# A linear-attention block followed by a multiplicative feed-forward block: PSUM banks split four and four, kv in quarters of the array, the second factor's pieces and the last block rearranged

## The chip, the cores and the metric

The kernel runs on one core of a Trainium2 chip. The time is device microseconds of one execution. Three runs of the kernel before gave 779.88, 779.91 and 781.03 us; the median is 779.91 us. The profile is of one further execution, whose instructions span 776.9 us (778.64 us as that run was timed). All sums here are made against that span.

## What is computed

For each of 8 batches and 8 heads, with 576 tokens and a head dimension of 64:

```
kv  = k^T v                      # 64 x 64 per head, summed over 576 tokens
o   = q kv                       # 576 x 64
x   = o / sqrt(mean(o*o) + 1e-6) * g_norm
```

The heads are put side by side, so that `x` is 4608 tokens by 512. Then, with w1 and w2 of 512 x 1024, w3 of 1024 x 1024 and w_out of 1024 x 512:

```
a = x w1;  b = x w2;  h = (a*b) w3;  out = h w_out
```

All inputs and the result are float32 in value; the weights come in a wider format and are converted on the chip.

## The kernel before, in words

**Weights first.** `w3 w_out` doesn't depend on x, so the kernel multiplies it once (`turn_w3`, L579, and `fold_chunk`, L592; about 16 to 85 us of the span) and keeps the 1024 x 512 product in `w3o_sb`. While that runs, batch 0 of attention runs between the chunks.

**Groups of tokens.** 512 of each batch's 576 tokens form a group of their own; the 64 left over of all eight batches form a ninth group. The groups run in the order 0 to 6, 8, 7 (L1085). For each group T the gate products `x w1` and `x w2` are made in four passes (`gates`, L742), and then the projection by `w3o_sb`. Group 0 projects with one level of Winograd's scheme for 2 x 2 blocks (`project`, L766); every later group with two levels (`project_twice`, L854), which needs the second factor's blocks in seven pieces, with their own sums.

**The second factor's pieces.** `prepare_b` (L795) makes these seven pieces once, during the gates of group 1, four VectorE subtractions for each, staged in one of the two output tiles `o_sbs`, and stores each by two DMAs into a scratch tensor in DRAM (`w3o_l2`). Piece 6 is stored once more by itself, unsummed, for use at the very end (L799). `load_b` (L823) fetches pieces again, for every group, into one of three stream buffers. `between` (L1089) is called twice in each gate pass and makes two pieces each time.

**One pass of gates** is `winograd` (L610): seven products of 4 float32 matmuls each, in PSUM banks r1, r2 and r3. ScalarE copies banks out (`keep`, L628) as `p1`, `p5`, `u2`, `u3`; VectorE adds banks to those and multiplies the two halves (`multiply`, L747). Their order is: r1 for p1, r2 for p5, r1 again for u2; `between`; r2 again for block c12; r1 again for u3; r3 for c11; `between`; r1 a fourth time for c21. So r1 is given back only when c21 has been read. For c21, ScalarE copies half of the bank (L752) and VectorE multiplies by the other half, read from PSUM (L753). The next pass may take r2 only if a bank is free.

**Attention between the products.** `steps` (L516) is a list of eight steps for the next batch; `between` runs one of them. In one step, `begin_kv` (L477) makes kv for two pairs of heads (`kv`, L315), and `finish` makes the attention product of the two pairs before (L396), with squares on ScalarE, a sum over heads on VectorE, a square root on ScalarE and a reciprocal and a multiplication on VectorE (`norm`, L371). From batch 2 on, q and x are transposed by DMA (`turn_by_dma`, L267): GpSimd copies the words apart (L284, L286), SP's queue issues the transpose (L288), and GpSimd puts them together (L298). kv of one pair is 8 matmuls with 128 tokens as rows and 64 columns (L326), two heads in the two halves of the array's columns, and 2 more for the 64 tokens left over, whose tile is padded with zeros to 128 rows. Four ScalarE copies put the result into `kv_sb` twice (L337), since the product needs it on both halves of the partitions.

**Order of the work.** PE, GpSimd and SP run in the order in which the program is written. VectorE and ScalarE are put in order by the scheduler outside some stretches that are fixed by hand (L1000, L1110). Each engine and each DMA queue keeps its own order, so an instruction that waits holds all those behind it.

**PSUM.** Eight banks: five rotate for products (`ps_mm`, L75), three for attention and transposes (`ps_at`, L76).

**The end** (L951 to L986, last group): products 0 to 6 of the second level. `finish` (L904) is four VectorE additions; `add` (L927) adds PSUM banks to a kept tile by two VectorE additions; `last_block` (L933) finishes the block before, multiplies by the unsummed piece and stores the last quarter in two parts. The tiles called u2 and u3 share one buffer (L608).

Of the kernel before, what the change touches and what calls it, by code (L numbers as in the profile page):

```python
# [21 lines left out]
def kernel(  # L22
# [42 lines left out]
    J = 4  # L65
# [6 lines left out]
    const = ctx.enter_context(tc.tile_pool(name="const", bufs=1))  # L72
    inp = ctx.enter_context(tc.tile_pool(name="inp", bufs=2))
    work = ctx.enter_context(tc.tile_pool(name="work", bufs=2))
    ps_mm = ctx.enter_context(tc.tile_pool(name="ps_mm", bufs=5, space=PSUM))  # L75
    ps_at = ctx.enter_context(tc.tile_pool(name="ps_at", bufs=3, space=PSUM))  # L76

    conv_pool = ctx.enter_context(tc.tile_pool(name="conv", bufs=1))

# [2 lines left out]
    def bank(pool, tag):  # L82
        return pool.tile([P, 512], FP32, name=tag, tag=tag)
# [2 lines left out]
    loaded = {}  # L86
    q_left = {}

    kv_left = [const.tile([P, H, D], FP32, name=f"{name}l_sb") for name in "kv"]

    def load_pair(names, b, r):

# [9 lines left out]

    def load_kv_left(b):
        for t, src in zip(kv_left, (k, v)):
            nc.sync.dma_start(out=t[0:L], in_=src[b, :, G:S, :].rearrange("h p d -> p h d"))

    def load_q_left(b):
        if b % 2 == 0:
# [137 lines left out]

    ident = const.tile([P, P], FP32, name="ident")
    make_identity(nc, ident)
    for t in kv_left:
        nc.gpsimd.memset(t[L:P], 0.0)  # L250
    eps_col = const.tile([P, 1], FP32, name="eps_col")
    nc.vector.memset(eps_col, 1e-6)

# [6 lines left out]

    def keep_warm(n):

        t = bank(ps_mm, "mm")
        for _ in range(n):
            nc.tensor.matmul(t[:, 0:P], lhsT=ident, rhs=ident, start=True, stop=True)

# [41 lines left out]
    def attention(b):  # L308
# [6 lines left out]
        def kv(rs):  # L315


            n = len(rs)
            kv_ps = bank(ps_at, "at")[:, 0:n * D].rearrange("p (r d) -> p r d", d=D)
            for r in rs:  # L320
                k_sb, v_sb = loaded["k", b, r], loaded["v", b, r]
                kl, vl = kv_left
                for j in range(J + 1):
                    cols = slice(j * D, (j + 1) * D)
                    for e in range(2):
                        nc.tensor.matmul(  # L326
                            kv_ps[e * D:(e + 1) * D, r - rs[0], :],
                            lhsT=k_sb[:, e, cols] if j < J else kl[:, 2 * r + e, :],
                            rhs=v_sb[:, e, cols] if j < J else vl[:, 2 * r + e, :],
                            start=(j == 0),  # L330
                            stop=(j == J),
                        )
            for e in range(2):
                for i in range(2):
                    dst = kv_b[i * D:(i + 1) * D, e, rs[0]:rs[0] + n, :]
                    src = kv_ps[e * D:(e + 1) * D]
                    nc.scalar.copy(dst, src)  # L337

        def q_t(r):

# [401 lines left out]
    def gates(T, p, between, ready=lambda name: None):  # L742
        def done(name, one, two):
            multiply(name, one, two)
            ready(name)

        def multiply(name, one, two):  # L747

            dst = ab[int(name[1]) - 1][:, p, int(name[2]) - 1, :]
            if two is None:  # L750
                c = late_pool.tile([P, N], FP32, name="c21")
                nc.scalar.copy(c, one[:, 0, :])  # L752
                nc.vector.tensor_mul(dst, c, one[:, 1, :])  # L753
                return
            c = late_pool.tile([P, 2, N], FP32, name="c")
            nc.vector.tensor_add(c, one, two)  # L756
            nc.vector.tensor_mul(dst, c[:, 0, :], c[:, 1, :])  # L757

        winograd(
            lambda name, w, c: wa[p][name][:, w, c, :],  # L760
            lambda name, c: xb[T][name][:, c, :],
            NP // 2, done, between,
        )
# [30 lines left out]

    def prepare_b():  # L795

        for n, y in enumerate(b_blocks()):
            if n == 6:
                nc.sync.dma_start(  # L799
                    out=w3o_l2[7, :, 0:1024].rearrange("p (f n) -> p f n", n=N), in_=y  # L800
                )
            b11, b12, b21, b22 = (
                y[:, 2 * i:2 * i + 2, j * P:(j + 1) * P] for i in range(2) for j in range(2)
            )

            stage = o_sbs[n % 2].rearrange("p m n -> p (m n)")[:, 0:6 * P]
            t1, t2, t4 = (t.rearrange("p (c n) -> p c n", n=P) for t in (
                stage[:, i * 2 * P:(i + 1) * 2 * P] for i in range(3)
            ))
            nc.vector.tensor_sub(t1, b12, b11)  # L810
            nc.vector.tensor_sub(t2, b22, t1)
            nc.vector.tensor_sub(b12, b22, b12)
            nc.vector.tensor_sub(t4, b21, t2)
            nc.sync.dma_start(
                out=w3o_l2[n, :, 0:1024].rearrange("p (f n) -> p f n", n=N), in_=y
            )
            nc.sync.dma_start(out=w3o_l2[n, :, 1024:PART], in_=stage)
            yield
# [35 lines left out]
    def project_twice(T, last, ahead):  # L854
# [43 lines left out]
        def keep(name, ps):  # L898
            t = late_tile(name)
            nc.scalar.copy(t[:, 0:4], ps[0])  # L900
            nc.scalar.copy(t[:, 4:7], ps[1][:, 0:3])
            return t
# [27 lines left out]

        done[T] = len(done)

        def last_block(z):  # L933

            a22, t4 = ab[1][:, :, 1], loaded_b[7 * done[T] + 6]
            t4 = t4.rearrange("p (f n) -> p f n", n=N)
            finish(z, 1, 0)
            ps = bank(ps_mm, "mm").rearrange("p (m n) -> p m n", m=2)
# [29 lines left out]
        sum_inner(5)  # L968
        finish(z, 0, 1)
        products(4, r1)  # L970
        z = keep("u3", r1)
        load_b()
        if not last:
            sum_inner(6)
        nc.vector.tensor_add(p5, p5, z)
        finish(p5, 1, 1)
        products(5, r2)
        load_b()
        add(p1, r2)
        finish(p1, 0, 0)  # L980
        if last:
            last_block(z)
        else:
            products(6, r1)
            load_b()
            finish(keep("u4", r1), 1, 0)  # L986
# [99 lines left out]
    for n, T in enumerate(groups):  # L1086
        pieces = steps(T + 1) if n + 2 < NG else iter([])

        def between():  # L1089
            next(pieces, lambda: None)()  # L1090
            if T == 1:
                for _ in range(2):
                    next(preparing, None)
                if len(loaded_b) == 0 and next(preparing, 0) == 0:
                    for _ in range(3):
                        load_b()

# [69 lines left out]
```

## Time and profile before

| what | value |
|---|---|
| runs | 779.88, 779.91, 781.03 us |
| span of the profiled execution | 776.9 us |
| PE | 761.9 us, 98% of the span, 5775 records |
| VectorE (DVE) | 542.0 us, 70% |
| ScalarE (ACT) | 249.5 us, 32% |
| GpSimd (POOL) | 135.1 us, 17% |
| mean clock granted to PE | 0.996 |

A busy share is the time in which an engine had an instruction running. A row of the timeline reads: start, duration, engine, line and operation, out<-in by the program's names, shape, count, and in brackets the idle time of the engine before it and what ended it. "ACTq" and "SPq" are queues that issue DMAs. A float32 matmul leaves two records on PE, a transpose one.

### The profile page before, as it was taken

How to read it: one execution, taken by the hardware profiler on the slowest of the kernel's cores; microseconds unless marked ns; L12 is line 12 of the kernel's file. 1: busy time of each engine (PE TensorE's matmuls, PEld its weight loads, DVE VectorE, ACT ScalarE, POOL GpSimd, SP SyncE). 2: the span in 40 equal slices, each digit the busy share in tenths (PEclk: the TensorE clock that was granted, in tenths of full speed). 3: DMA queues.
4: the chain of work that ended last, by engine and by line, in shares of the span. 5: the costliest groups of instructions: out<-in, count | busy, mean ns of one | idle time of the engine just before them, and what ended most of it. 6: DMA issues, size and time to landing. Idle time of an engine off the chain costs nothing.

```text
span 776.9 us, 14423 instructions
## 1 busy us (share of the span) xinstructions
PE 761.9 (98%) x5775; PEld 660.9 (85%) x5775; DVE 542.0 (70%) x1086; ACT 249.5 (32%) x483; POOL 135.1 (17%) x132
## 2 busy tenths in 40 slices
PE   8999999999979999999999999999999999999997
PEld 6455788888869889988998899889988998898896
DVE  6978999439579567945784778567756864594566
ACT  6687643212212332232222322332133222122120
POOL 0000000221330253033204520331144000000000
PEclk9999999999999999999999999999999999999999
DMA  9996650238998844884388448734852470074014
GB/s 316 339 331 182 200 149 30 82 102 260 243 290 281 223 99 109 282 231 110 90 281 220 109 117 271 220 95 133 271 108 51 138 249 0 1 244 143 1 57 167
DMA packets 132775, 132.55 MB, mean 171 GB/s; under 512 B 76644, under 2 KB 120676, under 8 KB 132708
## 3 DMA queue, kind: packets, MB, share of 16 engines
q1 hardware_dynamic: 130256, 116.81, 51.1%
q10 hardware_dynamic: 2452, 14.81, 5.5%
q8 instruction: 46, 0.75, 0.4%
q14 instruction: 21, 0.17, 0.1%
HBM read 100.27 MB, written 16.38 MB: 150 GB/s over the span
## 4 chain that ended last, share of the span: by engine, by line
PE 89%; DVE 5%; DMA 3%; SPq 1%; ACT 1%; issue 1%; POOL 0%; DVEq 0%; ACTq 0%; POOLq 0%
PE mm L617 55%; PE mm L889 21%; PE mm L596 7%; PE at L326 2%; PE at L409 2%; DMA raw<-in_moe_w_out_dram 1%; PE at L583 1%; SPq L288 1%; DVE c L756 1%; DMA w3o_l<-raw 1%; DMA xn<-xT 1%; PE at L345 1%; DVE ab L757 0%; DMA raw<-in_moe_w_dram 0%; DMA out_dram<-raw 0%
## 5 line engine op out<-in xcount | busy, mean ns | idle before, releaser
L617 PE MATMUL mm<-xT,w_sb 128*128 128x256 f32 x768 | 176.2, 379 | 0.0
L617 PEld LDWEIGHTS mm<-xT,w_sb 128*128 128x128 f32 x768 | 145.5, 190 | 20.0 <-issue 0.5
L617 PE MATMUL mm<-xc,ws 128*128 128x256 f32 x576 | 132.2, 382 | 4.9 <-ACT p L630 4.9
L617 PEld LDWEIGHTS mm<-xc,ws 128*128 128x128 f32 x576 | 110.2, 192 | 20.8 <-ACT p L630 5.7
L756 DVE TENSOR_TENSOR c<-mm,u 128x512 f32<-128x512 f32 x36 | 24.9, 691 | 105.8 <-PE mm L617 105.8
L630 ACT COPY u<-mm 128x512 f32<-128x512 f32 x74 | 43.4, 587 | 141.6 <-PE mm L617 133.3
L630 ACT COPY p<-mm 128x512 f32<-128x512 f32 x74 | 43.3, 587 | 87.9 <-PE mm L617 78.5
L617 PE MATMUL mm<-xc,w_sb 128*128 128x256 f32 x288 | 69.3, 383 | 0.0
L889 PE MATMUL mm<-w3o_sb,raw 128*128 128x128 f32 x500 | 62.3, 275 | 0.6 <-DVE raw L849 0.6
L596 PE MATMUL mm<-chunks,ab 128*128 128x512 f32 x128 | 60.2, 601 | 1.7 <-DVE chunks L165 1.6
L617 PE MATMUL mm<-xT,ws 128*128 128x256 f32 x256 | 61.3, 382 | 0.0
L284 POOL COPY xT<-xn 128x1024 uint16<-128x1024 uint16 x26 | 32.3, 1271 | 162.2 <-DVE xn L387 162.1
L617 PEld LDWEIGHTS mm<-xc,w_sb 128*128 128x128 f32 x288 | 53.6, 190 | 7.8 <-ACT u L630 0.3
L757 DVE TENSOR_TENSOR ab<-c 128x256 f32<-128x256 f32 x108 | 58.0, 537 | 3.0
L889 PEld LDWEIGHTS mm<-w3o_sb,raw 128*128 128x128 f32 x500 | 59.0, 192 | 0.9 <-DVE raw L849 0.8
L617 PEld LDWEIGHTS mm<-xT,ws 128*128 128x128 f32 x256 | 48.3, 191 | 6.8
L378 DVE TENSOR_REDUCE inv<-sq 128x8 f32<-128x512 f32 (+1 forms) x40 | 23.4, 626 | 36.0 <-ACT sq L377 36.0
L756 DVE TENSOR_TENSOR c<-p,u 128x512 f32<-128x512 f32 x36 | 25.6, 711 | 27.6 <-ACT u L630 27.4
L889 PE MATMUL mm<-w3o_sb,ab 128*128 128x128 f32 x336 | 43.8, 275 | 0.3 <-DVE ab L851 0.3
L889 PEld LDWEIGHTS mm<-w3o_sb,ab 128*128 128x128 f32 x336 | 41.0, 192 | 0.8 <-DVE ab L851 0.5
L596 PEld LDWEIGHTS mm<-chunks,ab 128*128 128x128 f32 x128 | 21.9, 190 | 22.7 <-issue 15.8
L900 ACT COPY u<-mm 128x512 f32<-128x512 f32 x23 | 13.5, 587 | 85.4 <-DVE raw L913 64.7
(157 smaller groups left out, 1138.7 us busy)
## 6 DMA issues: line engine op xcount, KB each, us to landing
w3o_sb<-w3o_l SPq DMA_DIRECT2D x26, 896.0 KB, 5.0
raw<-in_moe_w_dram SPq DMA_DIRECT2D x31, 512.0 KB, 7.3
raw<-w3o_l SPq DMA_DIRECT2D x13, 896.0 KB, 5.1
w3o_sb<-w3o_l ACTq DMA_DIRECT2D x11, 896.0 KB, 4.7
k_sb<-in_k_dram SPq DMA_DIRECT2D x32, 256.0 KB, 3.7
v_sb<-in_v_dram SPq DMA_DIRECT2D x32, 256.0 KB, 4.3
q_sb<-in_q_dram SPq DMA_DIRECT2D x32, 256.0 KB, 4.2
out_dram<-raw SPq DMA_DIRECT2D x14, 512.0 KB, 3.5
```

The costliest lines, as they stand in the source:

```text
L284: nc.gpsimd.tensor_copy(to, src.rearrange("p a n w -> p w a n"))
L288: nc.sync.dma_start_transpose(out=turned.bitcast(U16).rearrange("p (a t) -> p a t", t=P), in_=apart.bitcast(U16))
L326: nc.tensor.matmul(kv_ps[e * D:(e + 1) * D, r - rs[0], :], lhsT=k_sb[:, e, cols] if j < J else kl[:, 2 * r + e, :], rhs=v_sb[:, e, cols] i ...
L378: nc.vector.tensor_reduce(out=inv[:, i], in_=sq.rearrange("p (h d) -> p h d", d=D), axis=AX.X, op=ALU.add)
L409: nc.tensor.matmul(o_ps[l][tokens, n * D:(n + 1) * D], lhsT=qT[r][rows, e, i, tokens], rhs=kv_b[rows, e, r, :], start=True, stop=True,)
L596: nc.tensor.matmul(sums_ps[half][m], lhsT=w3T[half, c][:, m, :], rhs=chunks[:, c, 1, :], start=(c == 0), stop=(c == KF - 1),)
L617: nc.tensor.matmul(ps[:, u, :], lhsT=lhsT(a_name, u, c), rhs=rhs(b_name, c),  start=(u == 0 and c == 0 and to is None), stop=(c == chunks ...
L630: nc.scalar.copy(t, ps)
L756: nc.vector.tensor_add(c, one, two)
L757: nc.vector.tensor_mul(dst, c[:, 0, :], c[:, 1, :])
L889: nc.tensor.matmul(to[:, i, :], lhsT=x[:, c, :], rhs=y[:, c, :], start=new and place // 4 not in seen, stop=(c == 1), skip_group_check=True,)
L900: nc.scalar.copy(t[:, 0:4], ps[0])
```

## The change

- **PSUM**: four banks for products, four for attention. The matmuls that keep PE warm at the start and the last block take banks of attention.
- **kv**: the tiles of left-over tokens hold heads in two halves of the partitions (4 DMAs for each batch in place of 2, no padding with zeros, half the size). From batch 1 on each matmul takes 64 tokens and 64 columns, a quarter of the array: the two halves of the 128 partitions go to two PSUM banks. The left-over tokens come after all others and use one half of the rows. ScalarE copies the first bank to `kv_sb`, VectorE adds the second bank there, ScalarE copies the sum to the other half of the partitions. In batch 0 the 128-row matmuls stay, and only the left-over tokens use 64 rows.
- **c21**: ScalarE copies the whole bank, VectorE multiplies the halves of the copy.
- **Pieces of the second factor**: piece 6's unsummed store goes first; the staging tile is chosen otherwise (piece 4 is staged in the place of the first sum, which is piece 1; 0, 2 and 5 in one output tile, 1, 3 and 6 in the other); the three first loads are spread over two calls of `between`.
- **The end**: the bank of product 4 is added to p5 straight from PSUM, ahead of its copy to u3; the block made of u3 is finished ahead of product 5, no longer after it.

```diff
-    ps_mm = ctx.enter_context(tc.tile_pool(name="ps_mm", bufs=5, space=PSUM))
-    ps_at = ctx.enter_context(tc.tile_pool(name="ps_at", bufs=3, space=PSUM))
+    ps_mm = ctx.enter_context(tc.tile_pool(name="ps_mm", bufs=4, space=PSUM))
+    ps_at = ctx.enter_context(tc.tile_pool(name="ps_at", bufs=4, space=PSUM))
...
         for t, src in zip(kv_left, (k, v)):
-            nc.sync.dma_start(out=t[0:L], in_=src[b, :, G:S, :].rearrange("h p d -> p h d"))
+            for i in range(2):
+                heads = src[b, i * H // 2:(i + 1) * H // 2, G:S, :]
+                nc.sync.dma_start(out=t[i * L:(i + 1) * L], in_=heads.rearrange("h p d -> p h d"))
...
-    for t in kv_left:
-        nc.gpsimd.memset(t[L:P], 0.0)
...
+            halves = 2 if b else 1
...
             for r in rs:
-                for j in range(J + 1):
+                for j in range(J):
...
+                    for h in range(halves):
+                        rows = slice(h * P // halves, (h + 1) * P // halves)
+                        for e in range(2):
+                            k_in, v_in = (loaded[name, b, r][rows, e, cols] for name in "kv")
+
+                            add(h, r, e, k_in, v_in, r == rs[0] and j == 0, False)
+            for r in rs:
+                i = r // 2
+                for e in range(2):
+                    k_in, v_in = (t[i * L:(i + 1) * L, r % 2 * 2 + e, :] for t in kv_left)
+                    add(i % halves, r, e, k_in, v_in, False, True)
             for e in range(2):
...
+                if halves == 2:
+
+                    nc.scalar.copy(dsts[0], srcs[0])
+                    nc.vector.tensor_add(dsts[0], dsts[0], srcs[1])
+                    nc.scalar.copy(dsts[1], dsts[0])
...
-                c = late_pool.tile([P, N], FP32, name="c21")
-                nc.scalar.copy(c, one[:, 0, :])
-                nc.vector.tensor_mul(dst, c, one[:, 1, :])
+                c = late_pool.tile([P, 2, N], FP32, name="c21")
+                nc.scalar.copy(c, one)
+                nc.vector.tensor_mul(dst, c[:, 0, :], c[:, 1, :])
...
+        nc.sync.dma_start(
+            out=w3o_l2[7, :, 0:1024].rearrange("p (f n) -> p f n", n=N), in_=b_blocks()[6]
+        )
         for n, y in enumerate(b_blocks()):
-            if n == 6:
-                nc.sync.dma_start(
-                    out=w3o_l2[7, :, 0:1024].rearrange("p (f n) -> p f n", n=N), in_=y
-                )
...
-            stage = o_sbs[n % 2].rearrange("p m n -> p (m n)")[:, 0:6 * P]
+            stage = w3o_sums[0].rearrange("p f n -> p (f n)") if n == 4 else (
+                o_sbs[(n - n // 5) % 2].rearrange("p m n -> p (m n)")
+            )
+            stage = stage[:, 0:6 * P]
...
         products(4, r1)
+        if last:
+
+            add(p5, r1)
         z = keep("u3", r1)
         load_b()
         if not last:
             sum_inner(6)
-        nc.vector.tensor_add(p5, p5, z)
+            nc.vector.tensor_add(p5, p5, z)
         finish(p5, 1, 1)
+        if last:
+
+            finish(z, 1, 0)
         products(5, r2)
...
                 for _ in range(2):
-                    next(preparing, None)
-                if len(loaded_b) == 0 and next(preparing, 0) == 0:
-                    for _ in range(3):
+                    if next(preparing, 0) == 0 and len(loaded_b) < 3:
                         load_b()
```

More of the change, by code (lines that the diff above doesn't have):

```diff
@@ L87 @@
     q_left = {}
-    kv_left = [const.tile([P, H, D], FP32, name=f"{name}l_sb") for name in "kv"]
+    kv_left = [const.tile([P, H // 2, D], FP32, name=f"{name}l_sb") for name in "kv"]
     def load_pair(names, b, r):
@@ L261, in keep_warm @@
     def keep_warm(n):
-        t = bank(ps_mm, "mm")
+        t = bank(ps_at, "at")
         for _ in range(n):
@@ L318, in kv, with add @@
             n = len(rs)
-            kv_ps = bank(ps_at, "at")[:, 0:n * D].rearrange("p (r d) -> p r d", d=D)
+            halves = 2 if b else 1
+            kv_ps = [
+                bank(ps_at, "at")[:, 0:n * D].rearrange("p (r d) -> p r d", d=D)
+                for _ in range(halves)
+            ]
+            def add(h, r, e, k_in, v_in, start, stop):
+                nc.tensor.matmul(
+                    kv_ps[h][e * D:(e + 1) * D, r - rs[0], :], lhsT=k_in, rhs=v_in,
+                    start=start, stop=stop, skip_group_check=True,
+                )
@@ L320, in kv @@
             for r in rs:
-                k_sb, v_sb = loaded["k", b, r], loaded["v", b, r]
-                kl, vl = kv_left
-                for j in range(J + 1):
+                for j in range(J):
                     cols = slice(j * D, (j + 1) * D)
[L325 to L331, printed above, removed]
-                        )
@@ L333, in kv @@
-            for e in range(2):
[L334 to L337, printed above, removed]
+                    for h in range(halves):
[3 more added lines that the diff above has]
+                            add(h, r, e, k_in, v_in, r == rs[0] and j == 0, False)
@@ new lines, in kv @@
+            for r in rs:
[3 more added lines that the diff above has]
+                    add(i % halves, r, e, k_in, v_in, False, True)
+            for e in range(2):
+                dsts = [kv_b[i * D:(i + 1) * D, e, rs[0]:rs[0] + n, :] for i in (e, 1 - e)]
+                srcs = [t[e * D:(e + 1) * D] for t in kv_ps]
+                if halves == 2:
+                    nc.scalar.copy(dsts[0], srcs[0])
+                    nc.vector.tensor_add(dsts[0], dsts[0], srcs[1])
+                    nc.scalar.copy(dsts[1], dsts[0])
+                else:
+                    for dst in dsts:
+                        nc.scalar.copy(dst, srcs[0])
@@ L795, in prepare_b @@
     def prepare_b():
+        nc.sync.dma_start(
+            out=w3o_l2[7, :, 0:1024].rearrange("p (f n) -> p f n", n=N), in_=b_blocks()[6]
+        )
         for n, y in enumerate(b_blocks()):
-            if n == 6:
-                nc.sync.dma_start(
-                    out=w3o_l2[7, :, 0:1024].rearrange("p (f n) -> p f n", n=N), in_=y
-                )
             b11, b12, b21, b22 = (
@@ L804, in prepare_b @@
             )
-            stage = o_sbs[n % 2].rearrange("p m n -> p (m n)")[:, 0:6 * P]
+            stage = w3o_sums[0].rearrange("p f n -> p (f n)") if n == 4 else (
+                o_sbs[(n - n // 5) % 2].rearrange("p m n -> p (m n)")
+            )
+            stage = stage[:, 0:6 * P]
             t1, t2, t4 = (t.rearrange("p (c n) -> p c n", n=P) for t in (
@@ L931, in project_twice, with last_block @@
         done[T] = len(done)
-        def last_block(z):
+        def last_block():
             a22, t4 = ab[1][:, :, 1], loaded_b[7 * done[T] + 6]
             t4 = t4.rearrange("p (f n) -> p f n", n=N)
-            finish(z, 1, 0)
-            ps = bank(ps_mm, "mm").rearrange("p (m n) -> p m n", m=2)
+            ps = bank(ps_at, "at").rearrange("p (m n) -> p m n", m=2)
             for m in range(2):
@@ L981, in project_twice @@
         if last:
-            last_block(z)
+            last_block()
         else:
```

## Prediction

> **What bounds the kernel now.** I read the page first: PE is busy for 761.9 of 776.9 us. Then PE's own waits, since only what makes PE wait, lengthens PE's work or lies after its last matmul can move the end.
>
> ```profile
> PE mm L617 <- ACT p L630: 4.9, 2, 4.3
> ```
>
> Of 9.4 us of waits in all, this row holds 4.9 us, in two waits. The longest is in the gates of group 1. The timeline around it shows what stood behind it:
>
> ```profile
> 208.91 0.57 SPq L799 DMA_DIRECT2D w3o_l<-raw  x1
> ...
> 212.02 0.42 DVE L812 TENSOR_TENSOR raw<-raw 128x256 f32<-128x256 f32 x1 [5.70 <-DMA w3o_l<-raw]
> ...
> 213.49 1.29 DVE L387 TENSOR_TENSOR xn<-at,inv 128x512 f32<-128x512 f32 x2 [1.04 <-POOL xT L298]
> ...
> 217.43 1.07 ACT L630 COPY p<-mm 128x512 f32<-128x512 f32 x2 [6.71 <-DVE c L756]
> ...
> 218.07 3.50 PE L617 MATMUL mm<-xc,ws 128*128 128x256 f32 x8 [4.31 <-ACT p L630]
> ```
>
> The reader is to see one chain. The unsummed store of piece 6 (L799) stands on SP's queue behind two DMA transposes that are issued from 204.65 us on. VectorE stood 5.70 us until it landed, then 1.04 us for GpSimd's copy out of the same transposes, and all that was queued behind came late: the c11 addition, ScalarE's copy of p1, PE. The eight records at 218.07 take 3.30 us to the next row's start (221.37) where others take 1.73.
>
> **What the Trainium skill says.** "TensorE: Matmul & The Clock Gate", Part 1, says that an idle window of about 3.4 us puts PE at half its clock. The trace agrees: after the idle 4.31 us the granted clock is 0.5 for 3.41 us, which loses half of that, 1.7 us. After the other wait (0.57 us, at 186.7) it isn't lowered. "TensorEngine Tiling (Array Packing)", Tiling Modes, says that a change of tiling mode drains the engine. The chain of waits, in order of time, agrees:
>
> ```profile
> 46.98 0.44 PE at L583 x4
> ...
> 49.01 0.59 PE at L345 x4
> ...
> 588.32 1.09 PE at L409 x64
> ```
>
> Four transposes cost 0.44 us among full-array work, 0.59 us after kv: 0.15 us for the change. kv of 10 matmuls takes 0.73 us and of 20 1.31 us: 0.058 each and 0.15 to enter. Quarter-array matmuls, 16 in 0.62 us (L427) and 32 in 1.09 us (L409), take 0.029 each and again 0.15, whether after kv or, as in the row shown, after full-array work. "PSUM — Partial Sum Buffer", PSUM bank collisions, says that the compiler keeps two engines off one bank even for reads; the trace doesn't show it, but in the changed program the copy to u3 waits for VectorE's reads of that bank.
>
> **The change part by part.**
>
> *Pieces (group 1).* In the new program's order SP issues the unsummed store ahead of all pieces, and the q loads and both x transposes stand ahead of the stores of pieces 4 to 6, no longer behind them; these stores had waited for VectorE until 201.6 us. Moving 3 loads of batch 3's k, v and left-over tokens ahead of pieces 2 and 3 costs nothing: they waited for PE alone since 179.6. So the x transposes go from 204.65 to about 197 to 201 (behind GpSimd's copy of the q transposes, which themselves go from 189.6 to about 185), GpSimd is done by about 206, and VectorE can go on at about 207 where it went on at 213.49. Then 1.28 (xn), 0.7, 1.1 and 0.7 (the L756 and L757 rows) end near 211, ahead of 213.7 when PE needs p1. Both wait and clock loss go: -4.3 - 1.7 = -6.0. The waits of 0.58 and 0.30 us at 231 to 233, where VectorE's subtractions take 1.27 in place of 0.42 beside GpSimd's copies, may go as well as those come earlier: half, -0.4. The extra 0.57 us that L799 takes on SP at 177 is hidden, since VectorE doesn't wait for the next store before 199.
>
> *kv on PE.* A call from batch 1 on: 32 quarters and 4 left-over matmuls (two at a time) are 32 x 0.029 + 4 x 0.058 = 1.16 and 0.15 to enter, 1.31 as before. But 13 of the 14 calls are followed by L409 in the same mode: -0.15 x 13 = -1.95. Batch 0's four calls change mode once more: +0.6. Rounding 0.02 x 14: +0.3. Together -1.1; bounds -2.2 (left-over matmuls overlap) and +1.0 (no saving).
>
> *kv off PE.* ScalarE keeps four copies of 0.27 us, but the last two now wait for two VectorE additions that the trace doesn't have. L910, 128 elements, took 0.29: 0.28 each. On ScalarE squares, c21's copy and the square root are queued behind. In the group 2 to 6 steps at 262 to 566 us VectorE is free about 0.5 us after the first two copies; the chain comes 0.8 us later, and c21's copy had 0.82 us to spare. Nothing. In group 1 VectorE is held at 180.9 to 183.1 by two subtractions of 1.14 and 1.25 us; there c21's copy ends at about 185.7.
>
> *Four product banks.* r2 of a pass now takes the bank of r1 of the pass before, so PE waits for c21's copy, which grows from 0.38 to 0.59 us (the copy of L630). With 0.59 it would end 0.89 us before r2 in nearly all 36 passes: nothing. Exceptions: where c21's copy is queued behind the left-over tokens' square root.
>
> ```profile
> 281.29 2.97 PE L617 MATMUL mm<-xc,ws 128*128 128x256 f32 x13
> ...
> 281.50 0.30 ACT L382 ACTIVATE inv<-inv,eps_col 128x8 f32<-128x8 f32 x1 [3.00 <-DVE inv L378]
> 281.71 0.35 ACT L752 COPY c<-mm 128x256 f32<-128x256 f32 x1
> ```
>
> Here r2 started 0.4 us ahead of the copy. It will start at 281.71 + 0.59 + 0.05 = 282.35: +1.06. In the same place of group 4 (433.13 against 432.99): +0.78; in group 6 there are 0.52 us to spare. In group 1 r2 goes from 184.25 to about 185.75 (+1.5), which swallows the wait of 0.57 us after it: +1.0. In group 0 VectorE has hardly a gap from 85 to 135 us. Four kv additions (1.1 us) and four subtractions moved ahead put it 2.5 us back there; c21's copy at 114.08 goes to about 116.2 and r2 from 115.6 to 116.85, +1.25, and the copy of p1 adds 0.3: +1.5 (bounds 0 and 3). Together +1.0 + 1.8 + 1.5 = +4.3. No idle time here comes near 3.4 us.
>
> *The end.*
>
> ```profile
> 765.37 0.59 ACT L900 COPY u<-mm 128x512 f32<-128x512 f32 x1 [6.41 <-DVE raw L913]
> ...
> 766.37 1.09 DVE L975 TENSOR_TENSOR p<-p,u 128x896 f32<-128x896 f32 x1 [1.09 <-ACT u L901]
> ```
>
> From 766.37 to 773.99 VectorE has no gap, and PE is done at 771.3. VectorE waited 1.09 us for both copies to u3. Now it adds from PSUM at once (0.6 + 0.5 in place of 1.09), so all that follows comes 1.1 us earlier, and 0.18 us of dependency before L947 goes. But the store of block (0, 0), 256 KB, is now issued just ahead of the last two of 128 KB (1.9 us to landing), +0.4. Sum -0.9; bounds -1.3 and 0.
>
> *Hidden.* Bank changes at the start: PE is busy without a gap from 16 to 84.6 us. Two more loads a batch on SP: 0.4 us ahead of transposes that have 2 us and more.
>
> Sum: -6.4 - 1.1 + 4.3 - 0.9 = **-4.1 us**, a span of 772.8. The runs' median lies 3.0 us above the span, 779.91; I take the same offset: **775.8 us**. Within 0.2% (1.6 us) is about what can't be told from no change here.
>
> **The rivals.**
>
> *The banks cost nothing* (0.22). The waits at 114, 281 and 433 depend on where GpSimd's copies happen to hold VectorE; with the first moved and the passes rearranged they may vanish. The sum without most of the 4.3: 772.5. For it: 33 of 36 passes have 0.5 us or more to spare. Against: ScalarE's order there isn't changed.
>
> *The chain keeps its length* (0.16). If the x transposes land only 2 us earlier, GpSimd takes the place of the DMA: a wait of 2.3 us stays, without the lowered clock. Gain there 3.7 in place of 6.4: 778.5. For it: VectorE waited for GpSimd as well (1.04). Against: SP's queue is free of VectorE's stores by 197.
>
> *ScalarE blocked by the additions* (0.12, slower). One mechanism: ScalarE's last two kv copies wait for VectorE, and c21's copy behind them gives r2's bank back. From 0.9 us of delay on, every us is PE's. If that holds in the five steps of groups 2 to 6 as in group 1, at 1.5 us each: +7.5, 783.3. For it: group 1 shows such subtractions of 1.2 us. Against: at 264 to 568 us they are over when GpSimd starts.
>
> **How the numbers follow.** Forecast 0.50, rivals 0.22, 0.16, 0.12. Faster by over 0.2% (below 778.35): 0.48 + 0.20 + 0.05 = 0.73; within: 0.02 + 0.02 + 0.10 = 0.14; slower 0.01 + 0.12 = 0.13. The range leaves out the slower rival and the best ends of the bounds: 771.0 to 780.0.
>
> **What would show it.** PE's longest wait on ScalarE's p is gone and the clock is never 0.5 after the start; L799's successor delays no VectorE row; kv and L409 together take 2.25 us, not 2.40; PE waits of 0.8 to 1.5 us for c21's copy at three or four passes; VectorE's gap before the end is gone. A wait of over 3 us near 213 us, or waits on c21's copy in every group, would make me wrong.

## The result and the profile after

| | median | runs | span of the profiled execution |
|---|---|---|---|
| before | 780.47 us | 779.88 to 781.27 (4) | 776.9 us |
| after | 775.01 us | 774.11 to 775.83 (4) | 772.5 us |

The ratio is 0.9929, with a 95% interval of 0.9912 to 0.9946: 5.5 us less, 4.4 us in the profiled span. 775.8 and 772.8 were forecast, a change of 4.1 us. The head of the page of the changed kernel, and its rows for PE's waits:

```profile
span 772.5 us, 15381 instructions
...
PE 759.0 (98%) x6223; PEld 658.8 (85%) x6223; DVE 557.7 (72%) x1115; ACT 257.6 (33%) x483; POOL 133.6 (17%) x130
```

```profile
PE mm L636 <- ACT p L649: 2.6, 2, 1.8
...
PE at L446 <- POOL qT_left L298: 1.2, 1, 1.2
PE mm L912 <- DVE ab L874: 0.6, 1, 0.6
PE mm L636 <- DVE p L951: 0.5, 1, 0.5
```

The first row is the one that held 4.9 us before. It still holds 2.6 us, in two waits, but these are other waits: 1.8 us in group 0 and 0.8 us in group 1. The wait of 4.3 us at piece 6 is gone, as the timeline at that place shows:

```profile
205.28 2.25 POOL L298 COPY xT<-xn 128x1024 uint16<-128x1024 uint16 x2 [5.61 <-DMA xn<-xT]
...
208.60 1.28 DVE L406 TENSOR_TENSOR xn<-at,inv 128x512 f32<-128x512 f32 x2
209.80 0.68 DVE L776 TENSOR_TENSOR c<-p,u 128x512 f32<-128x512 f32 x1
...
211.75 0.69 DVE L776 TENSOR_TENSOR c<-mm,p 128x512 f32<-128x512 f32 x1
...
213.89 3.62 PE L636 MATMUL mm<-xc,ws 128*128 128x256 f32 x16
```

GpSimd is done at 207.5 us, VectorE normalises x without waiting, the additions that set p5 and p1 free (`c<-p,u` and `c<-mm,p`) are over at 212.4, and PE's two products at 213.89 follow each other without a gap and at full clock.

Where the time went can be read from PE alone: the start of the first product of each stage, and the differences. The table below is worked out in that way for all kernels whose stages the text speaks of (us; "other gates" are those of groups 3 to 8, "projections" all but the last).

| kernel | to the gates of 0 | gates 0 | gates 1 | gates 2 | other gates | projections | last projection to end |
|---|---|---|---|---|---|---|---|
| before | 84.61 | 58.23 | 60.65 | 54.38 | 311.26 | 179.75 | 27.95 |
| after | 84.75 | 60.21 | 54.29 | 55.54 | 310.19 | 180.35 | 27.18 |
| after, once more | 84.91 | 60.64 | 54.29 | 54.71 | 310.19 | 180.34 | 27.18 |
| banks alone | 84.17 | 58.52 | 60.81 | 54.38 | 311.26 | 181.08 | 27.95 |
| store first | 84.38 | 58.23 | 53.57 | 54.38 | 311.27 | 180.08 | 27.94 |
| two in a call | 84.07 | 58.23 | 55.60 | 54.38 | 311.26 | 179.15 | 27.95 |
| pieces alone | 84.25 | 58.28 | 53.55 | 54.38 | 311.27 | 178.76 | 27.94 |
| after, kv whole | 84.76 | 59.01 | 53.53 | 54.43 | 311.16 | 180.40 | 27.29 |
| after, loads later | 85.33 | 60.64 | 54.85 | 54.07 | 310.19 | 180.48 | 27.18 |
| after, old end | 84.95 | 60.11 | 54.29 | 55.45 | 310.19 | 180.84 | 27.94 |
| after, c21 by half | 85.62 | 60.67 | 54.29 | 54.61 | 310.19 | 180.71 | 27.18 |
| pieces and end | 84.33 | 58.35 | 53.56 | 54.38 | 311.26 | 180.14 | 27.17 |
| and quarters from 1 | 84.20 | 60.67 | 54.29 | 54.14 | 310.19 | 180.53 | 27.31 |
| and quarters from 4 | 84.54 | 58.23 | 53.55 | 54.29 | 310.19 | 180.74 | 27.17 |

The gates of groups 3 to 8 repeat to a few hundredths between kernels that share a part, and so mostly do those of group 1. Those of groups 0 and 2 do not always: in the two profiles of the changed kernel they differ by 0.43 and 0.83 us, for reasons that the runs below show. The first column and that of the projections vary by 1.5 and 2.3 us, by waits (for a load of weights, for VectorE) that stand at other places in each profile; 0.56 of the first is batch 0's kv in the changed kernel and its variants, the rest shows no pattern. So a part of the change is priced in its stage, and the total, which carries that scatter, tells only effects of a few us.

### The profile page after: what moved, and what is told of

Same layout as the page of the kernel before. It is cut to its first block, busy times and chain, and to the rows that moved or that the text cites. A ratio compares the mean times of both kernels' runs of the same rounds, so it can differ in the third digit from the quotient of the medians.

```text
span 772.5 us, 15381 instructions
## 1 busy us (share of the span) xinstructions
PE 759.0 (98%) x6223; PEld 658.8 (85%) x6223; DVE 557.7 (72%) x1115; ACT 257.6 (33%) x483; POOL 133.6 (17%) x130
## 4 chain that ended last, share of the span: by engine, by line
PE 82%; DVE 9%; DMA 5%; SPq 1%; issue 1%; ACT 1%; POOL 0%; DVEq 0%; ACTq 0%; POOLq 0%
PE mm L636 52%; PE mm L912 18%; PE mm L615 6%; PE at L327 2%; PE at L428 2%; DMA raw<-in_moe_w_dram 1%; DMA raw<-in_moe_w_out_dram 1%; DVE c L776 1%; SPq L288 1%; DMA w3o_sb<-w3o_l 1%; PE at L602 1%; DMA out_dram<-raw 1%; DVE ab L777 1%; DVE w_sb L167 1%; DVE ab L157 0%
## 5 line engine op out<-in xcount | busy, mean ns | idle before, releaser
L776 DVE TENSOR_TENSOR c<-p,u 128x512 f32<-128x512 f32 x36 | 27.5, 765 | 27.3 <-ACT u L649 27.3
L772 ACT COPY c<-mm 128x512 f32<-128x512 f32 x36 | 21.1, 587 | 68.9 <-PE mm L636 68.9
```

The lines of the kernel that those rows point to most:

```text
L772: nc.scalar.copy(c, one)
```

## The experiments

### Banks alone

The kernel before, with

```diff
-    ps_mm = ctx.enter_context(tc.tile_pool(name="ps_mm", bufs=5, space=PSUM))
-    ps_at = ctx.enter_context(tc.tile_pool(name="ps_at", bufs=3, space=PSUM))
+    ps_mm = ctx.enter_context(tc.tile_pool(name="ps_mm", bufs=4, space=PSUM))
+    ps_at = ctx.enter_context(tc.tile_pool(name="ps_at", bufs=4, space=PSUM))
```

and the warming matmuls and the last block in a bank of attention.

> The kernel before with four banks for products and four for attention, all else as it was (c21 multiplied out of its bank by VectorE). My theory after the changed kernel's trace: the banks are handed out in the order in which they came free, so the second product of a pass takes a bank that VectorE freed early, and not the one that c21 still holds. Then no wait of PE is added: within 0.5 us of the kernel before, and the first xc,ws product at 281.3 us starts where it did, before c21's copy. The rival is the prediction on record: the second product takes the first one's bank and waits for c21's copy and multiplication; then PE waits of 1 us or more appear at 281 and 433 us and the time is 2 to 3 us longer.

Measured: 780.05 us, ratio 1.0002 (0.9992 to 1.0011). The timeline of PE and ScalarE in group 2, at the place where the prediction put a wait:

```profile
281.52 3.62 PE L617 MATMUL mm<-xc,ws 128*128 128x256 f32 x16
...
281.80 0.35 ACT L752 COPY c<-mm 128x256 f32<-128x256 f32 x1
```

The second product (r2) starts at 281.52 us, before c21's copy out of the pass before has begun, and the gates of group 2 take 54.38 us as before. So r2 doesn't get the bank that c21 holds. The trace of the changed kernel agrees: from the third pass of group 0 on, r2's first matmul waits for a semaphore of VectorE in every pass and never for one of ScalarE, which alone reads c21's bank there. That fits banks that are given out in the order in which they come free (VectorE's additions free r2 and r3 before c21 frees r1). The prediction's largest single loss did not exist.

A small one that it had put under "hidden" did. The four sums of `fold_chunk` hold four banks for products until ScalarE has copied them to `w3o_sb`. Of five banks one was left for the first product of group 0; of four none is, and that product now waits for ScalarE's semaphore. In three profiles of the changed kernel's kind PE stands there (0.16, 0.35 and 0.52 us, put down to the copy into `w3o_sb`), and again for 0.32 to 0.35 us some 4 us later, for p1's copy. Here PE doesn't stand at the first product, but the gates of group 0 take 58.52 us, 58.23 to 58.35 with five banks; that this comes of the banks is likely and not shown. In the kernel with quarters from batch 4 on, which has four banks too, nothing is lost (58.23).

### After, c21 by half

The changed kernel, with

```diff
-                c = late_pool.tile([P, 2, N], FP32, name="c21")
-                nc.scalar.copy(c, one)
-                nc.vector.tensor_mul(dst, c[:, 0, :], c[:, 1, :])
+                c = late_pool.tile([P, N], FP32, name="c21")
+                nc.scalar.copy(c, one[:, 0, :])
+                nc.vector.tensor_mul(dst, c, one[:, 1, :])
```

> The changed kernel with c21 as before: ScalarE copies half of the bank and VectorE multiplies by the other half out of PSUM. Theory: the whole copy takes 0.21 us more of ScalarE and nothing waits for the bank; only where ScalarE is late itself is that seen: PE's wait at 119 us goes from 1.8 to about 1.6 us, and the time by 0.2 to 0.4 us, within what can't be told. Rival: the whole copy is what puts p1's copy late, and the waits in groups 0 and 1 go: 2 us less.

Measured: 774.09 us, ratio 0.9923 (0.9906 to 0.9940). PE's wait in group 0 is 1.76 us where it was 1.78, and in group 1 0.78 as before. The 0.21 us that I had put down to the longer copy are not seen either: c21's form costs and gains nothing that these runs tell.

### The pieces: the store first, two in a call, and both

The text ahead of the prediction says that the old calls made two pieces each time. They made three, since the old condition advanced the pieces as well: in the trace of before the stores stand as pieces 0 to 2 (177 to 185 us), 3 to 5 (194 to 203 us) and 6 (212 us). The new ones make two.

Store first, in the kernel before:

```diff
     def prepare_b():
+        nc.sync.dma_start(out=w3o_l2[7, :, 0:1024]..., in_=b_blocks()[6])
         for n, y in enumerate(b_blocks()):
-            if n == 6:
-                nc.sync.dma_start(out=w3o_l2[7, :, 0:1024]..., in_=y)
```

> The kernel before with the unsummed store of piece 6 issued ahead of all pieces; staging and the number of pieces in a call stay. Theory (two links in a row): VectorE's wait of 5.7 us for that store goes, but the x transposes stay behind the stores of pieces 3 to 5 on SP's queue (204.7 us), GpSimd's copy of what they bring still ends at about 213.4 us, and VectorE's normalisation of x and all behind it waits for that: PE's wait for p1 stays above 3 us, and the gain is 0 to 0.8 us. Rival (the store alone): PE's wait goes and the time falls by 5 to 6 us.

Two in a call, in the kernel before:

```diff
                 for _ in range(2):
-                    next(preparing, None)
-                if len(loaded_b) == 0 and next(preparing, 0) == 0:
-                    for _ in range(3):
+                    if next(preparing, 0) == 0 and len(loaded_b) < 3:
                         load_b()
```

> The kernel before with only the calls between the products changed: two pieces in each call, where the old condition made a third one, and the loads spread. Theory: what matters is that the x transposes come ahead of the stores that wait for VectorE. They are issued at about 200 us, GpSimd is done by 208, and PE's wait for p1 of 4.3 us shrinks below 1 us with the lowered clock gone: 4.5 to 6 us less. Rival: without the store put first VectorE waits in piece 6 for its landing as before (over 3 us), and half of the gain or less is seen.

Pieces alone is both of them and the new staging tiles, in the kernel before:

> The kernel before with the whole rearrangement of the pieces (store first, staging, two in a call, loads spread) and nothing else. Theory: it carries more than the whole gain, 6 us in the gates of group 1 and nothing elsewhere: about 774.3 us where the kernel before has 780.5, no PE wait above 0.7 us in 200 to 225 us and no lowered clock after the start. Rival: the banks or kv had a part in it, and 2 us or more of it are missing here.

Measured: store first 771.81 us, ratio 0.9898 (0.9883 to 0.9912); two in a call 772.44 us, 0.9911 (0.9895 to 0.9927); all pieces 770.57 us, 0.9885 (0.9871 to 0.9900), a larger gain than the 6 us that I had expected. In the first and the last, PE has no wait left in the gates of group 1, which take 53.6 us in place of 60.65; with two in a call, waits of 0.57, 0.25 and 0.41 us are left and they take 55.6.

My theory of two links fell. With the store first the x transposes were issued at 205.6 us, no earlier than before, and the gain was whole. VectorE in that kernel:

```profile
206.59 0.69 DVE L756 TENSOR_TENSOR c<-p,u 128x512 f32<-128x512 f32 x1 [0.27 <-ACT u L630]
...
208.12 0.68 DVE L756 TENSOR_TENSOR c<-mm,p 128x512 f32<-128x512 f32 x1
212.87 1.29 DVE L387 TENSOR_TENSOR xn<-at,inv 128x512 f32<-128x512 f32 x2 [4.07 <-POOL xT L298]
```

The same two additions in the kernel before:

```profile
214.69 0.68 DVE L756 TENSOR_TENSOR c<-p,u 128x512 f32<-128x512 f32 x1
...
216.65 0.69 DVE L756 TENSOR_TENSOR c<-mm,p 128x512 f32<-128x512 f32 x1
```

With the store first VectorE waits 4.07 us for GpSimd, where it was 1.04 before, and it costs nothing: without the store's wait in piece 6 the scheduler has put both additions, which free p5 and p1 (206.59 and 208.12), ahead of the normalisation of x that waits for GpSimd. Before, they stood behind it. So the wait for the unsummed store was the cause; the later transposes only mattered in the old order on VectorE. Two in a call reaches nearly the same in the other way: the x transposes go out at 195.5 us, GpSimd is early, and of the store's wait 1.22 us are left.

The price is also larger than the prediction's 6.0 us: 7.1. The wait of 4.31 us is 4.47 from the start of one product to that of the next (213.60 would have been due, 218.07 it was), the lowered clock 1.77, and the wait of 0.57 us at 186.7, which I had thought lost in a new one, goes too (0.73 from start to start): 6.97. In the kernel with the pieces alone the two waits in the projection of group 1 are gone as well, and that projection takes 22.48 us in place of 23.47.

The row of windows over the gates of group 1, of before and of pieces alone (PE busy first, granted clock third from the end):

```profile
167.84:228.49 60.65, 55.77 (x433) 47.95 (x432) 40.70 (x78) 15.65 (x34) 18.29 (x17) 0.97 0.93 270
```

```profile
167.52:221.07 53.55, 53.55 (x433) 46.94 (x432) 41.07 (x78) 15.82 (x34) 18.72 (x17) 1.00 0.99 298
```

The same 433 records fill their window wholly, at full clock.

### After, once more

> The changed kernel once more. Theory: all its waits come from its program order, so the same are seen again: 1.8 us for p1 in group 0 (119 us), 0.8 us in group 1 (189 us), about 1.2 us for the left-over q in group 2 (274 us). Rival: the wait in group 2 comes from DMA issues on SP that take 1.3 to 1.9 us at times in place of 0.6, by chance, and it is 0.5 us or more shorter or longer here.

Measured: 774.98 us, ratio 0.9934 (0.9919 to 0.9948). The waits in groups 0 and 1 are there again (1.80 and 0.78 us); the 0.43 us that group 0 takes more are the waits at its start named under "Banks alone". The one for the left-over q in group 2 is not there; 0.20 us are lost at 279.7 instead. The rival was right there: it comes and goes.

### After, loads later

The changed kernel, with the loads of left-over k and v put behind the q transposes from batch 2 on:

```diff
-                if r + 1 == NP and "k" in names:
+                if r + 1 == NP and "k" in names and b < 2:
                     load_kv_left(b + 1)
...
+            if more:
+                fs[2].append((load_kv_left, b + 1))
             turn(2, a.x_by_dma, 0)
```

> The changed kernel with the four loads of left-over k and v issued one step later from batch 2 on: behind the q transposes and ahead of the x transposes. Theory: four issues of 0.6 us each in place of two stood ahead of the q transposes and made GpSimd's copy of the left-over q late by 1.2 us for PE; that wait goes: 1.2 us less. Rival: the x transposes behind them come late instead, or SP's slow issues stay in the way: no change.

Measured: the gates of group 2 take 54.07 us, 0.31 less than before, which is just what kv in quarters saves there; no wait is left in them. That alone proves little, since the second profile of the changed kernel hasn't the wait for the left-over q either. The total, 775.37 us (ratio 0.9943, 0.9927 to 0.9958), shows no gain: in its profile the start took 0.6 us more than in that of after, and the gates of groups 0 and 1 0.4 and 0.6 us. The edit bears on group 1 too: its x transposes go out 31.1 us after the start of the gates, 29.8 in after, as the rival feared; that they cost the 0.6 us isn't shown. What makes the wait is seen in SP's queue, before and after:

```profile
265.14 0.66 SPq L105 DMA_DIRECT2D kl_sb<-in_k_dram  x1
265.85 0.71 SPq L105 DMA_DIRECT2D vl_sb<-in_v_dram  x1
266.66 4.62 SPq L288 DMA_TRANSPOSE q_sb<-qT  x2
```

```profile
259.34 1.26 SPq L95 DMA_DIRECT2D v_sb<-in_v_dram  x1
...
261.16 1.28 SPq L95 DMA_DIRECT2D v_sb<-in_v_dram  x1
262.48 2.61 SPq L107 DMA_DIRECT2D kl_sb<-in_k_dram  x2
265.14 1.27 SPq L107 DMA_DIRECT2D vl_sb<-in_v_dram  x2
266.51 2.63 SPq L288 DMA_TRANSPOSE q_sb<-qT  x2
...
272.81 1.15 POOL L298 COPY qT_left<-ql_sb 128x1024 uint16<-128x1024 uint16 x1 [0.87 <-DMA ql_sb<-qT_left]
...
274.01 0.79 PE L446 MATMUL at<-kv_sb,qT_left 64*64 64x64 f32 x32 [1.23 <-POOL qT_left L298]
```

Half the size doesn't halve the issue: each load holds the queue for 0.6 us as the full one did, and now and then for longer (one of the four here took 1.87). The four take 3.9 us where two took 1.4. But they are not alone: two loads of v ahead of them took 1.26 and 1.28 us in place of 0.47. By both the q transposes begin 18.9 us after the start of the gates, 14.7 before, and GpSimd's copy of the left-over q comes late for PE.

How late it may be can be read across the profiles. The transpose of the left-over q is issued 21.6 and 21.4 us after the start of the gates in the two with a wait of over 1 us (after 1.23, old end 1.14), 20.4 us in the one with 0.12 us (c21 by half), and 20.3 us or less in those with none: 20.3 in the second profile of the changed kernel, 18.8 with kv whole, where the four loads stand at the same place and took their usual 0.6 us each, 19.4 before. So four loads at their usual pace don't make PE wait; they take most of the room, and slow issues, of these loads or of others, take the rest. Why an issue is slow at times these runs don't show.

The Trainium skill, "Perfetto Trace Analysis", Optimizing DMA Performance, says that the slices of an issuing queue are the making of descriptors and not the data's way. The trace agrees in so far as the time didn't follow the bytes; it didn't follow the number of rows either (256 rows of 256 bytes in place of 512).

### After, kv whole

The changed kernel without quarters and so without VectorE's additions; the left-over tokens still use 64 rows:

```diff
-            halves = 2 if b else 1
+            halves = 1
```

> The changed kernel with kv on the whole array in every batch (only the left-over tokens use 64 rows), so without VectorE's additions. Theory: the additions put ScalarE's last two kv copies, the squares and the square root late, and p1's copy queued behind them: the PE waits of 1.8 us (119 us) and 0.8 us (189 us) go or shrink to 0.6. kv and the product of 64 by 64 take 2.25 to 2.4 us in place of 2.25. Together 0.5 to 2.3 us less than the changed kernel. Rival: quarters save PE what the prediction said (2 us and more in 13 calls), and the waits come from the order of the pieces: 0 to 2 us more.

Measured: 772.67 us, ratio 0.9923 (0.9893 to 0.9954), 2.3 us below the second measurement of after. The two intervals overlap, so the stages decide: the gates of groups 0 and 1 take 1.6 and 0.8 us less than in the second profile of after, the other gates 1.0 more. kv and the product take 2.39 us a call, not 2.25, so PE's saving is given up wholly. But the waits of 1.8 and 0.8 us on p1 are gone; one of 0.33 us at 88.8, at the start of group 0, is left. What they were is shown by the chain of waits of the changed kernel in group 0:

```profile
113.92 0.69 DVE c L776
114.61 0.20 DVE kv_sb L352
114.82 0.30 ACT kv_sb L353
115.16 0.29 DVE kv_sb L352
...
117.45 1.20 DVE inv L397 x2
118.67 0.31 ACT inv L401
118.98 0.48 ACT p L649
119.50 1.99 PE mm L636 x8
```

VectorE has no gap there; its first kv addition comes 3 us after ScalarE's first copy, ScalarE's second copies and squares wait for it, VectorE's sum of the squares comes late in turn, ScalarE stands at the square root, and p1's copy is queued behind that. The timeline of the same place shows which product waits:

```profile
115.83 1.89 PE L636 MATMUL mm<-xc,ws 128*128 128x256 f32 x8
...
116.78 0.59 ACT L772 COPY c<-mm 128x512 f32<-128x512 f32 x1
...
119.50 1.99 PE L636 MATMUL mm<-xc,ws 128*128 128x256 f32 x8 [1.78 <-ACT p L649]
```

r2 (115.83) runs before c21's copy (116.78). It is the third product, which needs r1 back from p1's copy, that stands. Without the additions ScalarE's square root and p1's copy come in time (116.77 and 116.99 us in that kernel), and PE doesn't stop.

### After, old end

The changed kernel, with the end of before (`add(p5, r1)` and the earlier `finish(z, 1, 0)` taken out, the bank's copy added, and the block finished in `last_block`).

> The changed kernel with the end of before: the bank of product 4 is added to p5 out of the copy in u3, and the block made of u3 is finished in the last block. Theory: VectorE waits 1.1 us for both copies to u3 again, the last group takes 76.3 us as before in place of 75.5: 0.8 to 0.9 us more than the changed kernel. Rival: the end is set by PE's last products or by the store, and nothing changes.

Measured: 775.98 us, ratio 0.9950 (0.9936 to 0.9964), and the last projection to the end takes 27.94 us, 27.18 in both profiles with the new end. VectorE's rows, first with the old end, then with the new:

```profile
763.30 1.09 DVE L998 TENSOR_TENSOR p<-p,u 128x896 f32<-128x896 f32 x1 [1.09 <-ACT u L924]
```

```profile
761.64 0.68 DVE L951 TENSOR_TENSOR p<-mm,p 128x512 f32<-128x512 f32 x1
762.24 0.55 DVE L952 TENSOR_TENSOR p<-mm,p 128x384 f32<-128x384 f32 x1
...
768.38 0.75 DVE L969 TENSOR_TENSOR raw<-raw,at 128x256 f32<-128x256 f32 x2
```

The idle 1.09 us is gone, and VectorE has no gap from 758.6 us to the last addition.

### Pieces and end, and quarters on top of them

Three kernels: the kernel before with the new pieces and the new end; the same with four and four banks and kv in quarters from batch 1 on; and from batch 4 on. In the last two the padded tile and kv on the whole array are kept for the batches before, the loads of left-over tokens of batches 4 to 7 stand behind the q transposes, and c21 stays as it was before. The edit of the last (with 1 in place of 4 in the other):

```diff
         def kv(rs):
+            if b < 4:
+                return kv_all_rows(rs)
```

> The kernel before with the rearranged pieces and the new end, and neither kv, nor the banks, nor c21 changed. Theory: the two gains lie in different groups and add up: the gates of group 1 as in the run with the pieces alone (53.6 us), the last group 0.8 us shorter. 0.7 to 0.9 us less than the pieces alone, about 769.8 us, and 5 us less than the changed kernel. Rival: the end gains only with the other parts (it needs the bank of attention for the last block): as the pieces alone, 770.6 us.

> Pieces and end as in the run of these two, and kv in quarters with VectorE's additions from batch 1 on with four and four banks; left-over tokens of batch 0 padded as before, the four loads of left-over tokens from batch 4 on put behind the q transposes. Theory: PE saves 0.155 us in each of 13 calls, 2.0 us, but in groups 0 and 1, where VectorE has no gap, the additions make p1's copy late by 1.8 and 0.8 us: 0 to 1.5 us more than pieces and end alone. Rival: 1 to 2 us less.

> The same, but quarters only from batch 4 on (groups 2 to 6), where VectorE is free. Theory: eight calls by 0.155 us are saved and no wait comes: 1.2 us less than pieces and end alone, about 768.6 us, and the gates of groups 3 to 5 take 0.31 us less each. Rival: the additions or the two more loads cost as much there as quarters save: no gain.

Measured: pieces and end 771.05 us, ratio 0.9892 (0.9875 to 0.9909); quarters from batch 1 on 773.56 us, 0.9921 (0.9906 to 0.9937); from batch 4 on 771.38 us, 0.9887 (0.9870 to 0.9905).

By stages each part does what was expected: the end takes 27.17 us, with the last block in a bank for products, quarters from batch 4 on save 1.15 us in the gates of groups 2 to 6 with no new wait, and from batch 1 on they cost 2.3 and 0.75 us in groups 0 and 1 again (waits of 1.75 and 0.78 us; some 0.5 of the 2.3 lies in the first products of group 0). In the totals only the last is seen: 2.5 us more than pieces and end, where I had expected 0 to 1.5. Against pieces alone (770.57 us) the end and the late quarters show no gain, where 0.8 and 2.0 us were expected: in these profiles the projections took 1.4 and 2.0 us more, by waits for the weights' loads and for VectorE at other places each time. Whether that is chance or goes with the edits, three profiles can't tell.

What is clear of that scatter: the kernel before with the new pieces alone, 770.57 us, is faster than the changed kernel, 775.0 us in both of its measurements (intervals 0.9871 to 0.9900 against 0.9912 to 0.9946 and 0.9919 to 0.9948). The rest of the change, taken together, loses 4 us; by the two profiles 1.6 us of that lie in the projections and 0.5 at the start (batch 0's kv), and the others in groups 0 to 2, as above, less the savings.

## Why the prediction was right, point by point

The total was right within 0.8 us (as a change: 4.1 us less forecast, 5.5 by the medians, 4.3 in the profiled stages), and that it came so close was luck. The sum was not right in its parts: one loss of 4.3 us was put to a wait that doesn't exist, and losses of together about that size came by paths that I had priced at nothing: 3.0 us on ScalarE's queue in groups 0 and 1, and in one of two profiles 1.4 us on SP's queue in group 2.

| step | predicted | measured | from |
|---|---|---|---|
| pieces, gates of group 1 | -6.0 | -7.1 | pieces alone |
| pieces, projection of group 1 | -0.4 | -1.0, or -0.1 | pieces alone; after |
| kv on PE | -1.1 | -1.5 | 13 x -0.155, 4 x +0.14 |
| kv off PE | 0 | +3.0 | waits in groups 0 and 1 |
| four product banks | +4.3 | 0; 0 to +0.5 at the start of group 0 | banks alone |
| two more loads a batch | 0 | +1.4, or 0 | SP's queue, group 2 |
| the end | -0.9 | -0.8 | old end |

- *Pieces.* Right in cause; in the gates of group 1 mis-sized by 1.1, for the reasons given there. On the way the x transposes went out at 199.7 us in the changed kernel (197 to 201 was forecast), the q transposes at 190.6, where 185 was forecast. Of the two links that I named (the store, then GpSimd's copy) only the first was needed. The guess for the projection isn't settled: both its waits went with the pieces alone (-1.0), but in the changed kernel another of 0.59 us stands there.
- *kv on PE.* The bounds held. A call and its product take 2.25 us, as "what would show it" said. The lost rounding (0.3) wasn't there. In batch 0 each of four calls costs 0.14 us more (1.37 against 1.23), the 0.6 that was priced. The timeline of the changed kernel in group 2 shows a call, from 281.84 to the next product at 284.09:

```profile
281.84 1.16 PE L327 MATMUL at<-v_sb,k_sb 64*64 64x64 f32 x64
...
284.09 1.99 PE L636 MATMUL mm<-xT,ws 128*128 128x256 f32 x8
```

  With kv whole the change of mode between kv and the product comes back, 2.39 us. This fits what the Trainium skill, "TensorEngine Tiling (Array Packing)", Tiling Modes, says: a change of tiling mode drains the engine.
- *Four product banks.* The step that failed: "r2 of a pass now takes the bank of r1 of the pass before, so PE waits for c21's copy." I counted banks round in the order in which the program asks for them; r2's bank is another one, freed by VectorE. All waits built on it (+1.06 and +0.78 in groups 2 and 4, +1.0 and +1.5 in groups 1 and 0) fall: in group 4 r2 started 0.3 us ahead of c21's copy and nothing happened. The rival that the banks cost nothing was right in that, though not in its total of 772.5, since other losses came.
- *kv off PE.* "Nothing in groups 2 to 6" held: other gates and group 2 with loads later save the full 0.155 us a call (311.26 to 310.19 us for 7 calls). In groups 0 and 1 the lateness of VectorE and ScalarE was forecast well (c21's copy at 116.2 us, it came at 116.78), but I asked only who waits for c21, not what stands behind it on ScalarE's queue: the square root, and p1's copy. Start to start the wait in group 0 is 1.94 us; group 1 loses 54.29 - 53.55 + 0.31 = 1.05. So the slower rival's mechanism was real, in the two groups where VectorE is full, and not in the five where the rival put it.
- *Two more loads.* "0.4 us ahead of transposes that have 2 us and more" was mis-sized: 1.2 us as a rule, 2.5 here. With two slow loads of v ahead it made a wait of 1.23 us, 1.40 from start to start.
- *The end.* Right: 0.8 of 0.9.

The terms measured in the gates, in batch 0's kv and at the end sum to -5.0 with the 1.4 of the profiled execution; the stages fell by 4.3. What is left over is +0.6 in the projections, +0.3 in the gates of group 0, most of it in its first products, and -0.4 at the start; the first and the last are within their scatter. The waits of 0.6 and 0.5 us around the projection of group 1, in four profiles of the changed kernel's kind and in none with the pieces alone, I didn't settle.

Of the five signs named, four came as written (no long wait at piece 6 and no lowered clock, no VectorE row held by the unsummed store, 2.25 us a call, no gap on VectorE at the end); the waits for c21's copy didn't come at all, which should have counted against the sum even though the total agreed.

## What to carry to other kernels

Price a wait with all that is queued behind it: the store of one piece held VectorE for 5.7 us, and what cost PE 7 us was two additions queued behind it, while a wait of 4.07 us with nothing urgent behind it cost nothing. An edit that takes work from the bounding engine and gives two short steps to two in-order engines in turn (copy, add, copy) paid here only in the stages where both have gaps; where VectorE was full, 0.31 us saved cost 1.9. And a total that agrees proves no sum: check each term in its own stage, where the gates of groups 3 to 8 repeat here to 0.02 us and the total of one kernel, as a rule, to 1 or 2 us from run to run.

## What the runs showed of the hardware that I had not expected

A load of 64 partitions by 4 heads (64 KB in rows of 256 bytes) holds SP's queue as long as one of 64 by 8 heads: 0.59 to 0.68 us as a rule against 0.61 to 0.71, and at times up to 1.9. So splitting this load in two doubled what stands ahead of the next transpose.
